# Shares of background conversion in a DeltaNet and feed-forward kernel, another PSUM ring for one unit's outputs, and another first activation

## The chip, the cores and the metric

The kernel runs on one core of a Trainium2 chip. It has five engines that matter here: PE (TensorE, matmuls), DVE (VectorE), ACT (ScalarE), POOL (GpSimd) and SP (SyncE, which only starts transfers here). Each runs its own instructions in order. The metric is the device time of one execution in microseconds (us), lower is better.

## What is computed

```python
# attention: q, k, v of (4, 8, 768, 48), beta of (4, 8, 768), float32
k_n = k / (np.linalg.norm(k, axis=-1, keepdims=True) + 1e-06)
for t in range(S):
    y[:, :, t] = np.einsum('bhd,bhde->bhe', q[:, :, t], state)
    v_old = np.einsum('bhde,bhd->bhe', state, kt)
    state = state + bt[:, :, :, None] * np.einsum('bhd,bhe->bhde', kt, vt - v_old)
# (B, H, S, D) -> (B*S, H*D) = (3072, 384), then the feed-forward
h = x @ w_in                                # w_in (384, 2048), float64
g = h * (1.0 / (1.0 + np.exp(-1.702 * h)))
out = g @ w_out                             # w_out (2048, 384), float64
```

The two weight matrices are given in double precision and converted to float32 by the kernel, as integer work on their raw words.

## The kernel before

The sequence is cut into 6 chunks of 128 positions; with 4 batches that makes 24 units. Within a chunk the recurrence is a triangular system: the kernel inverts its 32x32 diagonal blocks (`invert`, all on DVE) and solves the four blocks of a unit one after the other.

**Hops.** The first chunk's units 0 to 3 have no state yet. They are solved as two pairs, 0 and 1, then 2 and 3, in eight *hops* each (lines 1333 to 1342, the first run, and 1364 to 1370, the second run, whose hop 0 stands apart on line 1345). In a hop PE solves one block of one unit and multiplies what is already solved into the next block of the other; ACT copies both results out of PSUM; the next hop's PE work needs these copies. `gather` puts a unit's values into PSUM first. Between hops PE runs matmuls on constants (`warm`) or one step of the feed-forward (`feed`). `put_out` (line 1325) multiplies a unit's outputs (`queries`, `outputs`), has ACT copy them into `xT` (`leave`), and adds the new state on DVE (`state`).

**Conversion in the background.** Each piece of weight takes six operations (`conversion`, line 229): an AND on DVE, a Relu on ACT, then OR, another mask, and two multiplications on DVE. `conversions` interleaves a piece with the first operation of the next one. `fill(us)` (line 327) emits such operations until their planned costs (0.75, 0, 0.95, 0.7, 0.95, 0.95) reach the given sum. The costs are planned for 768 columns, as in the first pieces; later pieces have 512 or 384. The texts name the pieces by the kernel's own names: *in 0* to *in 3* and *in 6* to *in 11* are w_in, *out f* is rows f of w_out (out 4 and out 6 are pairs). After out 6 the same background generator emits `invert(1)`, the inversion for the next chunk, and then the rest of the conversions. Where a piece is finished, `fetches` may start the transfer of another one. The raw words of out 1 and out 2 are loaded by `fetch_out` on lines 1350 and 1351, after `put_out(pair[1])`; the transfers that bring the last rows into `xT` are issued in `copies` (line 805) and stand before them on SP.

**Order.** Instructions through `vec`, `act`, `pe`, `pool` and `sync` are pinned: they keep the program's order on their engine. Calls through `nc.gpsimd` and `nc.sync` may be placed freely.

**After the hops.** A loop of 25 steps (line 1397) has in each a `fill(1.0)` and one step of the feed-forward's first matrix for units 0 to 3 (`hidden`, six matmuls; every second step ends in one Gelu on ACT). At fixed steps it also normalizes keys of later units (`early`: a square on ACT, a sum on DVE, a power on POOL, a reciprocal on DVE, eight scalings on ACT). Then come the first eight row blocks of the second matrix (`both_written`), the wait for the inversion, and from line 1429 the slots: slot 3 solves unit 4's first block and takes the second half of `both_written`, which waits for converted pieces; slot 4 and all later ones follow.

**PSUM.** Before the slots the pools are `ps_moe` (ring *moe*: warm matmuls and the feed-forward), `ps_big`, `ps_seq` (ring *seq*) and `ps_acc` (ring *acc*), two banks each. `psV`, which `gather` fills, lies in *acc*.

Of the kernel before, what the change touches and what calls it, by code (L numbers as in the profile page):

```python
# [13 lines left out]
ACT = mybir.ActivationFunctionType  # L14
# [4 lines left out]
def kernel(  # L19
# [50 lines left out]
    ps_moe = ctx.enter_context(tc.tile_pool(name="ps_moe", bufs=2, space=PSUM))  # L70
    early_banks = ExitStack()
    ps_big = early_banks.enter_context(tc.tile_pool(name="ps_big", bufs=2, space=PSUM))
    ps_seq = early_banks.enter_context(tc.tile_pool(name="ps_seq", bufs=2, space=PSUM))
    ps_acc = early_banks.enter_context(tc.tile_pool(name="ps_acc", bufs=2, space=PSUM))
# [15 lines left out]
    def place(dst, n):  # L90

        return dst[n if n < B else n % 2] if dst is QP else dst[n % len(dst)]
# [3 lines left out]
    def segments(n):  # L96

        c, m = units[n]
        if n < B:
            return [(slice(0, C), m, slice(c * C, (c + 1) * C))]  # L100
        at = c * C + m // 2 * CH
        return [(slice(u * CH, (u + 1) * CH), m % 2 * 2 + u, slice(at, at + CH)) for u in range(2)]

    def load(n, pairs, dma=nc.sync.dma_start):
        for dst, src in pairs:
            for rows, b, t in segments(n):
                dma(  # L107
                    out=place(dst, n)[rows, :, 0:D],
                    in_=src[b, :, t, :].rearrange("h p d -> p h d"),
                )  # L110
# [24 lines left out]
    vec, act, pe, pool = Engine(nc.vector), Engine(nc.scalar), Engine(nc.tensor), Engine(nc.gpsimd)  # L135
# [11 lines left out]
    ident = cpool.tile([128, 128], F32, name="ident")  # L147
# [6 lines left out]
    def warm(n, after=None):  # L154
        ps = ps_moe.tile([128, 256], F32, tag="moe", name="ps_warm")
        if after is not None:
            after(ps[:, 0:1], 0.0)
        for _ in range(n):
            pe.matmul(ps, lhsT=ones[:, 0:128], rhs=ones, start=True, stop=True)

    table = cpool.tile([128, 1], F32, name="table")
    act.activation(table, ident[:, 0:1], ACT.Copy)

    w_out = cpool.tile([128, FC, DM], F32, name="w_out")

# [161 lines left out]
    def fill(us):  # L327
        while us > 0:
            us -= next(behind, us)
# [126 lines left out]
    def gram(n):  # L456

        return gram_whole(n) if n < B else gram_halves(n)
# [44 lines left out]
    def turn(n):  # L503
        kTs[n] = wk.tile([128, NP, 128], F32, tag="kT", name="kT", bufs=5)
        transposed(home(n), kTs[n])

    def load_diagonal(n, Nd, dma):

        b = units[n][1]
        dma(  # L510
            out=NT[b * NB * H : (b + 1) * NB * H].rearrange("d i k -> d (i k)"),
            in_=Nd.rearrange("(d r) -> d r", r=BS * BS),
        )
# [15 lines left out]
    def send_blocks(n, others=(), dma=sync):  # L529

        G = ready[n][2]
        Nd = dram.tile([H * C * BS], F32, tag="Nd", name="Nd", bufs=4)
        to = Nd.rearrange("(h p k) -> p h k", p=C, k=BS)
        for blk in range(NB):
            u = slice(blk * BS, (blk + 1) * BS)
            k = u if n < B else slice(blk % 2 * BS, (blk % 2 + 1) * BS)
            (beside if blk in others else dma)(out=to[u], in_=G[u, :, k])
        return Nd

    def load_diagonals(Nds):  # L540

        for b in range(B):
            load_diagonal(b, Nds[b], sync)
# [89 lines left out]
    def bank(name, shape=(128, H, D), big=False):  # L633
        if late:
            return one_bank(name)[:, 0 : H * D].rearrange("p (h d) -> p h d", h=H)
        from_, tag = (ps_big, "big") if big else (ps_seq, "seq")
        return from_.tile(list(shape), F32, tag=tag, name=name)
# [3 lines left out]
    class Step:  # L641
# [104 lines left out]
                )  # L746

        def queries(self):
            pool_, tag = (ps_acc, "acc") if self.n % 2 else (ps_seq, "seq")
            whole = [pool_.tile([128, 512], F32, tag=tag, name="psY") for _ in range(2)]  # L750
            self.psY = [w[:, 0:256].rearrange("p (s t) -> p s t", s=2) for w in whole]
            self.psS = whole[0][:, 256 : 256 + NP * D].rearrange("p (j d) -> p j d", j=NP)
            if self.c > 0:

                self.turned(
                    (0, 5, 4, 1, 2, 7, 6, 3),
                    lambda h: ST[self.rows(h), self.b, h // 2 * D : h // 2 * D + DP],
                    lambda h: self.QS[self.rows(h), h // 2, 0:128],
                    True,
                )  # L760
# [382 lines left out]
    def new_step(n):  # L1143
        if n >= len(units):
            return NoStep()
        steps[n] = (Step if n < B else Half)(n)
        return steps[n]

    def together(solves, belows):

        solves = [(X, blk) for X, blk in solves if X]
        belows = [(X, blk) for X, blk in belows if X]
        psU = bank("psU") if solves else None
        psRs = [bank("psR") if X.n >= B else None for X, blk in belows]
        for h in range(H):
            for X, blk in solves:
                X.solve(blk, h, psU)
            for (X, blk), psR in zip(belows, psRs):
                X.below(blk, h, psR)
        for X, blk in solves:  # L1160
            X.solved(blk, psU)
        for (X, blk), psR in zip(belows, psRs):
            X.rest(blk, psR)
# [133 lines left out]
    pair = [new_step(n) for n in range(B)]  # L1297
# [12 lines left out]
    Ndx = [send_blocks(n) for n in (B, B + 1)]  # L1310
# [6 lines left out]
    def hops(a, b):  # L1317

        yield [(a, 0)], []
        for blk in range(NB - 1):  # L1320
            yield [(b, blk)], [(a, blk)]
            yield [(a, blk + 1)], [(b, blk)]
        yield [(b, NB - 1)], []

    def put_out(s):
        s.queries()
        s.outputs(True, lambda: fill(1.7))
        steps.pop(s.n)

    path, later = hops(*pair[:2]), hops(*pair[2:])  # L1330
    for X in pair[:2]:
        X.gather()
    for i in range(2 * NB):
        together(*next(path))
        if i in (1, 3):
            turn(B + HB + i // 2)
        if i in (4, 5):
            gram(B + HB + i - 4)
            Ndx.append(send_blocks(B + HB + i - 4))
        if i < 2 * NB - 1:  # L1340
            warm(NU if i == 2 else NU // 2 if i in (1, 3, 4, 5) else 2 * NU // 3)
        fill(1.8)
    put_out(pair[0])
    load_diagonals(Ndx)
    together(*next(later))
    put_out(pair[1])
    for X in pair[2:]:
        X.gather()
    load(8, ((KN, k),), sync)
    for f in range(1, 3):  # L1350
        fetch_out(f)
# [5 lines left out]
    def feed(n=1):  # L1357
        for _ in range(n):
            while ffn and next(ffn[0], None) is None:
                ffn.pop(0)  # L1360
# [3 lines left out]
    for i in range(1, 2 * NB):  # L1364
        together(*next(later))
        if i < 4:
            warm(NU if i < 3 else NU // 2)
        if i > 2:
            feed()
        fill(1.8)  # L1370
    for s in pair[2:]:
        put_out(s)
        feed()
# [89 lines left out]
```

## Time and profile before

| | |
|---|---|
| median of 3 runs | 722.04 us (721.86 to 733.28) |
| the profiled execution, in all | 721.79 us |
| its span, first to last instruction | 720.1 us |
| mean granted PE clock over the span | 0.979 |
| busy PE, DVE, POOL, ACT | 678.0, 457.1, 256.1, 239.0 us |
| Gelu's table load, and the load at the start | 1.28 us each, at 98.11 and 0.80 us |
| first instruction of the background inversion | 126.53 us |

How to read it: times in the timeline are us from the first instruction. A line of the timeline gives the start, the length, the engine, the operation and its tiles as out<-in; in square brackets stands how long the engine had been idle and what released it. "PE busy" has modelled ends, so a busy PE may still wait a little. The profile gives line 123 for everything that is recorded through the helper `pinned`, so operations are told apart by their tiles: `VU<-psU` and `VU<-psV` are the two copies of a hop, `w_in<-w_in,low` or `w_out<-w_out,low` is the Relu of a conversion, and `raw` or the weight's own name as a source marks its other operations.

### The profile page before, as it was taken

How to read it: one execution, taken by the hardware profiler on the slowest of the kernel's cores; microseconds unless marked ns; L12 is line 12 of the kernel's file. 1: busy time of each engine (PE TensorE's matmuls, PEld its weight loads, DVE VectorE, ACT ScalarE, POOL GpSimd, SP SyncE). 2: the span in 40 equal slices, each digit the busy share in tenths (PEclk: the TensorE clock that was granted, in tenths of full speed). 3: DMA queues.
4: the chain of work that ended last, by engine and by line, in shares of the span. 5: the costliest groups of instructions: out<-in, count | busy, mean ns of one | idle time of the engine just before them, and what ended most of it. 6: DMA issues, size and time to landing. Idle time of an engine off the chain costs nothing.

```text
span 720.1 us, 20454 instructions
## 1 busy us (share of the span) xinstructions
PE 678.0 (94%) x8787; PEld 582.7 (81%) x8787; DVE 457.1 (63%) x869; ACT 239.0 (33%) x566; POOL 256.1 (36%) x267
## 2 busy tenths in 40 slices
PE   9289899987999999999999999999999999999997
PEld 7156788854568888898988988988988988989997
DVE  4799758996577498597597595795793892110000
ACT  2363565433233313323323333223323223122020
POOL 6085002310156652542642733623522403304032
PEclk9677999999999999999999999999999999999999
DMA  9896655224222313214114124223122111010100
GB/s 173 140 191 144 178 126 130 60 50 109 56 51 60 57 35 80 42 37 93 28 36 93 29 49 80 45 44 61 35 53 54 31 26 31 7 24 1 29 0 23
DMA packets 129179, 46.66 MB, mean 65 GB/s; under 512 B 118848, under 2 KB 123584, under 8 KB 129088
## 3 DMA queue, kind: packets, MB, share of 16 engines
q1 hardware_dynamic: 125280, 39.89, 27.2%
q0 software_dynamic: 2624, 5.07, 3.2%
q8 instruction: 69, 1.13, 0.7%
q10 hardware_dynamic: 1184, 0.39, 0.2%
q14 instruction: 22, 0.18, 0.1%
HBM read 33.13 MB, written 11.01 MB: 61 GB/s over the span
## 4 chain that ended last, share of the span: by engine, by line
PE 50%; DVE 32%; DMA 6%; issue 5%; ACT 4%; SPq 3%; POOL 0%; DVEq 0%; ACTq 0%; POOLq 0%
PE ph L123 22%; PE po L123 14%; DVE P L123 14%; DVE YB L123 7%; DVE NT L123 4%; PE four L123 4%; PE ps_warm L123 3%; PE psU L123 3%; DMA NT<-Nd 3%; DVE VU L123 2%; DVE w_out L123 2%; DMA Nd<-G 2%; PE psT L123 2%; SPq L123 2%; PE psR L123 1%
## 5 line engine op out<-in xcount | busy, mean ns | idle before, releaser
L123 PE MATMUL ph<-xT,w_in 128*128 128x256 f32 x1152 | 258.0, 381 | 0.0
L123 PEld LDWEIGHTS ph<-xT,w_in 128*128 128x128 f32 x1152 | 215.6, 190 | 30.4 <-DVE o L123 0.7
L123 PE MATMUL po<-w_out,gT 128*128 128x192 f32 (+1 forms) x720 | 139.7, 349 | 12.7 <-DVE o L123 5.4
L983 POOL TENSOR_TENSOR gT<-gT 128x512 f32<-128x512 f32 x80 | 105.1, 1323 | 102.7 <-ACT gT L123 68.1
L123 PEld LDWEIGHTS po<-w_out,gT 128*128 128x128 f32 x720 | 118.6, 191 | 26.7 <-issue 8.4
L123 DVE TENSOR_TENSOR P<-NT,YB 64x2 f32<-64x2 f32 (+9 forms) x200 | 124.0, 620 | 5.7
L123 ACT ACTIVATE gT<-ph 128x512 f32<-128x512 f32 x90 | 53.8, 598 | 143.4 <-PE ph L123 142.4
L123 DVE TENSOR_REDUCE YB<-P 64x2 f32<-64x2 f32 (+9 forms) x200 | 81.7, 409 | 6.9
L123 PE MATMUL po<-TW,gT 128*128 128x192 f32 x480 | 82.0, 328 | 0.8 <-ACT o L123 0.8
L123 PEld LDWEIGHTS po<-TW,gT 128*128 128x128 f32 x480 | 78.0, 190 | 1.8 <-ACT o L123 1.1
L849 POOL TENSOR_SCALAR_AFFINE_SELECT M<-M 64x512 f32<-64x512 f32 x40 | 29.9, 747 | 94.6 <-ACT M L123 93.4
L123 ACT COPY VU<-psU 32x384 f32<-32x384 f32 x96 | 45.2, 471 | 51.7 <-PE psU L123 42.0
L123 DVE TENSOR_TENSOR o<-o,po 128x192 f32<-128x192 f32 x40 | 13.8, 346 | 73.8 <-PE po L123 44.5
L123 DVE TENSOR_TENSOR VU<-VU,psR 32x384 f32<-32x384 f32 x40 | 22.1, 554 | 40.8 <-PE psR L123 40.1
L123 DVE TENSOR_TENSOR NT<-NT,bL 64x1024 f32<-64x1024 f32 (+1 forms) x9 | 12.0, 1333 | 46.7 <-DMA NT<-Nd 46.7
L107 POOL DMA_DIRECT2D KN<-in_k_dram x24 | 17.0, 712 | 68.7 <-PE four L123 68.7
L123 DVE TENSOR_TENSOR VU<-VU,four 128x384 f32<-128x384 f32 x19 | 10.5, 551 | 45.8 <-issue 33.3
L346 POOL TENSOR_TENSOR rn<-ssq,half 128x8 f32<-128x8 f32 x12 | 22.2, 1846 | 47.6 <-DVE ssq L123 47.6
L123 PEld LDWEIGHTS psU<-VU,XB 32*32 32x32 f32 x1536 | 27.4, 105 | 13.7 <-issue 9.4
L123 ACT COPY xT<-four 128x256 f32<-128x256 f32 (+1 forms) x40 | 13.2, 330 | 76.1 <-DVE ST L123 73.7
L123 PE MATMUL ps_warm<-ident 128*128 128x256 bf16 x235 | 35.3, 310 | 2.1 <-POOL low L123 1.4
L123 ACT COPY M<-four 128x512 f32<-128x512 f32 x19 | 11.2, 587 | 78.7 <-DVE VU L123 69.9
(133 smaller groups left out, 786.7 us busy)
## 6 DMA issues: line engine op xcount, KB each, us to landing
QP<-in_q_dram SPq DMA_DIRECT2D x40, 96.0 KB, 2.8
VU<-in_v_dram SPq DMA_DIRECT2D x40, 96.0 KB, 3.6
out_dram<-o SPq DMA_DIRECT2D x40, 96.0 KB, 2.2
raw<-in_moe_w_out_dram SPq DMA_DIRECT2D x9, 384.0 KB, 3.8
NT<-Nd SPq DMA_DIRECT2D x24, 128.0 KB, 2.7
XB<-Yd SPq DMA_DIRECT2D x24, 128.0 KB, 2.6
Yd<-NT SPq DMA_DIRECT2D x22, 128.0 KB, 2.1
Nd<-G SPq DMA_DIRECT2D x86, 32.0 KB, 1.7
```

Source lines behind the costliest of these rows:

```text
L107: dma(out=place(dst, n)[rows, :, 0:D], in_=src[b, :, t, :].rearrange("h p d -> p h d"),)
L123: return lambda *a, **kw: tc.keep_in_program_order(op(*a, **kw))
L346: nc.gpsimd.tensor_tensor(rn, ssq, half, op=ALU.pow)
L849: nc.gpsimd.affine_select(out=M, in_=M, compare_op=ALU.is_gt, fill=0.0, base=0, pattern=[[0, H], [1, CH]], channel_multiplier=-1,)
L983: (engine or nc.gpsimd).tensor_tensor(o, a, b, op=op)
```

## The change

Four edits:

- the first activation, on a one-column tile called `table`, is Gelu where it was Copy;
- unit 1's output banks come from the ring *moe* (unit 3's stay in *acc*, units 0 and 2's in *seq*);
- `gather` of units 2 and 3 stands before the second run's hop 0 and before unit 1's output, where it stood behind both;
- `fill` is asked for 2.1 in each hop of the first run (1.8 before), for 2.7 in each of the hops 1 to 7 of the second run (1.8 before), and for 1.9 on each side of the second run's hop 0 (nothing before).

```diff
-    act.activation(table, ident[:, 0:1], ACT.Copy)
+    act.activation(table, ident[:, 0:1], ACT.Gelu_apprx_sigmoid)
...
         def queries(self):
-            pool_, tag = (ps_acc, "acc") if self.n % 2 else (ps_seq, "seq")
+            pool_, tag = (
+                (ps_moe, "moe") if self.n == 1 else (ps_acc, "acc") if self.n == 3
+                else (ps_seq, "seq")
+            )
...
             warm(NU if i == 2 else NU // 2 if i in (1, 3, 4, 5) else 2 * NU // 3)
-        fill(1.8)
+        fill(2.1)
     put_out(pair[0])
-    load_diagonals(Ndx)
-    together(*next(later))
-    put_out(pair[1])
     for X in pair[2:]:
         X.gather()
+    load_diagonals(Ndx)
+    fill(1.9)
+    together(*next(later))
+    fill(1.9)
+    put_out(pair[1])
     load(8, ((KN, k),), sync)
     for f in range(1, 3):
         fetch_out(f)
...
         if i > 2:
             feed()
-        fill(1.8)
+        fill(2.7)
     for s in pair[2:]:
         put_out(s)
         feed()
```

## The prediction, made before the changed kernel was run

> **What bounds it now.** I first cut the span into five stages with the busy-time table (stretch, length, then busy us of PE, weight load, DVE, ACT and POOL, granted clock, DMA share, GB/s).
>
> ```profile
> 0.00:65.20 65.20, 45.63 (x389) 34.71 (x389) 50.51 (x103) 26.27 (x63) 36.48 (x67) 0.79 0.92 170
> 65.20:110.07 44.87, 42.01 (x964) 33.83 (x963) 29.86 (x53) 27.10 (x57) 1.42 (x2) 1.00 0.57 139
> 110.07:162.03 51.96, 48.74 (x300) 38.32 (x297) 47.61 (x98) 24.70 (x67) 13.13 (x10) 1.00 0.36 80
> 162.03:185.97 23.94, 17.87 (x136) 9.64 (x136) 16.65 (x37) 7.09 (x13) 1.42 (x2) 0.93 0.35 90
> 185.97:720.00 534.03, 523.74 (x7005) 466.18 (x7004) 312.43 (x579) 153.80 (x366) 203.61 (x188) 1.00 0.21 43
> ```
>
> Stage two is the hops, three the feed-forward's first half beside the inversion, four the wait for the last conversions. From 185.97, where slot 4 solves, PE is busy 98%: the change touches nothing there, so a shift at slot 4 should arrive whole at the end. Stages three and four leave PE idle 3.2 + 6.1 = 9.3 us; that, and DVE's 15.0 idle us of stage two, are what earlier conversion could use.
>
> Then the chain of waits, stages two and three (start, length):
>
> ```profile
> 97.63 0.47 ACT VU L123
> 98.11 1.28 ACT L123
> 99.41 0.61 ACT gT L123
> 100.03 0.47 ACT VU L123
> ...
> 126.53 1.23 DVE NT L123
> ```
>
> The nameless step is Gelu's table load, ahead of two copies of the hops. At 126.53 the inversion starts; until 162 DVE's chain leads.
>
> Last, the timeline by engine, for what a hop waits on. ACT, DVE, SP, and the landing time of the first of the two `raw` loads:
>
> ```profile
> 69.66 0.60 ACT L123 ACTIVATE kT<-psT 128x512 f32<-128x512 f32 x1
> 70.64 0.48 ACT L123 COPY VU<-psU 32x384 f32<-32x384 f32 x1 [0.39 <-PE psV L123]
> 71.02 0.47 ACT L123 COPY VU<-psV 32x384 f32<-32x384 f32 x1
> 71.62 0.73 ACT L123 ACTIVATE w_in<-w_in,low 128x512 int32<-128x512 int32 x1
> ...
> 71.17 0.41 DVE L123 TENSOR_SCALAR w_in<-gT 128x512 int32<-128x512 int32 x1
> ...
> 87.29 3.77 SPq L123 DMA_DIRECT2D xT<-last  x6
> 91.15 1.80 SPq L123 DMA_DIRECT2D KN<-in_k_dram  x2
> 93.00 1.09 SPq L123 DMA_DIRECT2D raw<-in_moe_w_out_dram  x2
> DMA to landing us min/median/max: 3.9/3.9/3.9
> ```
>
> Each conversion has one Relu on ACT, between DVE's first and second operation, and ACT runs in order with the hop's copies. DVE lags PE here: the operation that feeds this Relu ends at 71.58, though the hop's solve was over at 70.56.
>
> **The change, part by part.** I counted `fill`'s planned costs through the program for both versions, which gives the operations in each hop, and laid the four queues out with the durations of these rows. The old order laid out so reaches slot 4 within 1.5 us of the trace; below, trace times plus the difference.
>
> *First run of hops, 2.1 for 1.8.* The Relu of piece in 6 moves from hop 2 into hop 1, ahead of hop 2's copies. It can't start before 71.62 and takes 0.73, so the copies start at 72.4, not 70.64: 1.7 later, of which 0.35 was slack behind the warm matmuls: +1.4. Two later Relus cost 0.2. Put-out 0 starts 1.6 late.
>
> *Gather, ring and the two fills of 1.9.* The gather's 1.5 us are only moved; its wait for unit 1's copies (0.64 in the trace) goes, as unit 1's outputs now hold the other ring. In its place two Relus stand ahead of the second run's hop 0 copy (0.7) and of unit 1's leaving copies (1.2), each waiting for DVE. The warm matmuls of its hop 1, which share that ring, now wait for unit 1's state sum on DVE: queued behind them is hop 2's solve, 1.4 to 2.2 late. The leaving copies come 3.2 late.
>
> *The fetch.* Those copies release the six `xT` transfers on SP, and behind them stand KN and the two `raw` loads of w_out rows 1 and 2: 5.7 us from the first to the `raw` load, by the rows. So it issues at 96.2 instead of 93.0 and lands 3.9 later, at 100.1. Before, piece out 1 was first touched at 102.54, long after landing. Now the 2.7 of the second run's hop 2 asks for it at 94.2: DVE stands 5.9 us, its Relu 5.7, and the copies of the second run's hop 3, queued behind on ACT, start at 101.1 instead of 94.38. PE sits 4.0 us. This is the largest term; if the data were there it would be nothing, so 0 and +4.0 are its ends. I take 4.0, for every step of it has a row.
>
> *The table.* Loaded at the start, where one load of 1.28 stands already. ACT ran Relu, Square and Copy after the second load without a third, so that set holds them. It saves 1.28 on ACT, of which about 0.8 stays on this path. The Trainium skill (ScalarE: Activation LUTs, What ACT_TABLE_LOAD costs) prices a switch at about 2.66 us, 1.38 of it a drain; here Gelu starts 0.02 after the load, so the trace shows no drain behind it. By the Trainium skill's figure the forecast would be some 1.4 us lower.
>
> *End of the hops:* unit 2 leaves at 112.6 instead of 106.77, **+5.8**.
>
> *The inversion.* By then the conversions are eleven us further. From 100.1 DVE has 17.1 us of operations left before the inversion (the ends of out 0 and 1, 2.35 each for out 2 and 3, 4.1 for each pair, state sums), 1.2 of collisions with POOL's subtractions (the 128x768 row at 118.00 took 1.38 against 0.69 elsewhere) and 2.0 of waits for Relus: start at 120.5, **6.0 earlier**.
>
> *But PE needs that less.* From 115.9 PE has its 25 remaining hidden steps (1.3 each, 36 matmuls took 7.77) whatever DVE does. And the early normalizations keep their places in the loop, now behind the inversion: unit 8's reciprocal comes after ten of its steps, 120.5 + 7.4 + 0.5 = 128.4, where ACT scaled at 119.79 before. Behind its 1.93 stands a Gelu that frees PE's bank: PE waits 2.5 us at the second hidden layer; other waits shrink by 0.4. Last Gelu: 150.75 + 5.8 + 2.1 = 158.7. Eight pairs of products (10.0) bring slot 3's solve to 169.3, where 162.03 was set by the inversion: **+7.3**.
>
> *The second half* had 23.94 us, most of it PE waiting for conversions. Now pieces 8, 13, 9 and 10 are done; four are left, the first behind a Relu queued after slot 3's copies. 2.9 for solve, copies and Relu; 9.1 for the rest of four conversions, 1.6 for two V sums, 1.6 of waits; 3.0 from the last conversion to slot 4 as before: 18.2, **-5.7**.
>
> Sum: +7.3 - 5.7 = +1.6 at slot 4. The profiled execution took 721.79 (span 720.1 and 1.7 around it), the median 722.04: **723.5**.
>
> **Rivals.** *The data is there (720.0).* If SP reaches the loads earlier, or `fill`'s work falls a step later than I counted, DVE never stands. The hops end at +2.0, inversion starts 10 early, slot 3 solves at 165.5 and slot 4 at 184.0: -2.0. For it: SP had a wait inside those rows that I can't place. 0.27.
>
> *Conversions fit the hops' gaps (714).* If no Relu delays a copy, the gather's wait and the table come off (0.6 + 0.8), inversion starts ten us earlier, and most of the 9.3 idle us of PE is collected: 6 to 8 in all. Against it: the row at 71.17. 0.15.
>
> *PE goes cold (727).* In the first stage PE stopped at 21.4 and the granted clock fell to 0.50 from about 24.5; after idling between 166 and 172 it was 0.50 in 172 to 174. A 4.0 us stand at 98 to 102 lies beyond the 3.1 that sufficed. Half clock for 3.5 us (as there) to 7 us (as after 35) costs 1.7 to 3.5 in matmul-bound hops: 725.2 to 727. It decides from a stand of about 3 us with no warm matmul in it. The Trainium skill (TensorE: Matmul & The Clock Gate, Part 1) says the clock halves after at least one idle window of about 3.4 us whose phase runs free. By that rule the trace agrees, and 4.0 us would only sometimes hold a whole window. Short matmuls around the stand speak against it. 0.18.
>
> That the change doesn't do what it says is possible for the table alone, worth 0.8.
>
> **Numbers.** Forecast 0.40, the rivals as given. The range runs from 715, near the collected case, to 729: 727 and 2 for what the layout misses (its error on the old order was 1.5). A difference of 2%, 14.4 us, is about what a measurement can tell from no change; none of the cases reaches it, the best by 6 us and the worst by 9. Unseen effects, such as SP transfers that are placed freely in the slots: 0.04 faster, 0.91 within, 0.05 slower.
>
> **What would show it.** One table load, at the start. The first run's hop 2 copies near 72.4; the `raw` loads on SP near 96; a stand of DVE and ACT of 5 to 6 us on out 1; the second run's hop 3 copies near 101. Inversion near 120.5 and slot 3 near 169: if it solves by 163 the third stage was mis-sized. Slot 4 at 187 to 188 and 534 us behind it. Wrong altogether if stage five changes length by over 2 us.

## The result, and the profile after

| | before | after |
|---|---|---|
| median | 721.86 us | 729.28 us |
| lowest | 719.22 us | 725.92 us |
| profiled execution, in all | 721.79 us | 727.72 us |
| its span, mean granted clock | 720.1 us, 0.979 | 726.0 us, 0.971 |

The medians are over 20 executions each. The ratio is 1.0112, with a 95% interval of 1.0078 to 1.0146: slower by 7.4 us by the medians and by some 8 by the ratio, where 1.5 were forecast, and just outside the range. Nearly every kernel of this case has some executions that lie 5 to 15 us above its lowest, with a lower mean granted clock, how many they are differs from kernel to kernel, and the ratios leave the longest of them out.

First the busy time by stage, cut at the same events as before (the hops' first solve, the hidden step behind unit 3's output, the solves of slots 3 and 4), with the same columns:

```profile
0.00:63.83 63.83, 43.42 (x390) 33.63 (x390) 49.58 (x102) 26.19 (x63) 35.35 (x67) 0.79 0.91 171
63.83:118.39 54.56, 45.58 (x963) 36.15 (x963) 39.55 (x70) 28.27 (x60) 4.06 (x4) 0.91 0.54 132
118.39:171.72 53.33, 49.14 (x300) 38.21 (x296) 43.19 (x93) 22.96 (x65) 11.13 (x8) 1.00 0.41 88
171.72:192.30 20.58, 17.29 (x138) 9.49 (x137) 12.55 (x27) 5.84 (x11) 1.54 (x2) 0.92 0.17 49
192.30:726.00 533.70, 524.12 (x7005) 466.26 (x7004) 312.41 (x579) 153.49 (x366) 203.79 (x188) 1.00 0.21 43
```

The hops (second row) grew by 9.7 us, and of that only 3.6 is PE work; the rest PE stood. The granted clock there is 0.91 where it was 1.00. The third row grew by 1.4, the fourth shrank by 3.4, the fifth is the same within 0.4 us. So the loss is in the hops, and the gain in the fourth stage does not pay for it.

The chain of waits in the second run of hops (start, length):

```profile
95.66 4.93 DMA raw<-in_moe_w_out_dram
100.61 0.37 DVE w_out L123
101.00 0.62 ACT w_out L123
101.64 0.47 ACT VU L123
...
104.16 2.86 PE ph L123 x6
...
122.56 1.23 DVE NT L123
```

This is the predicted path link by link: the late load of out 1, DVE's first operation on it, its Relu, and only then the copies of hop 3. New is the last-but-one link: a hidden step of six matmuls took 2.86 us, and the six of the next step took 1.49 at 107.95. The timeline of DVE and ACT shows how long each stood (in brackets), and of SP when the load was issued:

```profile
100.61 0.36 DVE L123 TENSOR_SCALAR w_out<-raw 128x384 int32<-128x384 int32 x1 [7.31 <-DMA raw<-in_moe_w_out_dram]
101.00 0.62 ACT L123 ACTIVATE w_out<-w_out,low 128x384 int32<-128x384 int32 x1 [7.96 <-DVE w_out L123]
101.64 0.47 ACT L123 COPY VU<-psU 32x384 f32<-32x384 f32 x1
...
95.66 1.09 SPq L123 DMA_DIRECT2D raw<-in_moe_w_out_dram  x2
```

Why matmuls took twice as long is in the windows of 2 us (same columns as the stages; the clock is the third figure from the end):

```profile
68.00:70.00 2.00, 0.65 (x48) 0.65 (x52) 1.97 (x3) 1.87 (x4) 0.00 (x0) 0.93 0.18 24
70.00:72.00 2.00, 2.00 (x38) 1.45 (x29) 1.97 (x4) 0.71 (x1) 0.00 (x0) 0.50 0.63 118
72.00:74.00 2.00, 2.00 (x55) 1.34 (x53) 1.93 (x4) 0.85 (x3) 0.00 (x0) 0.72 1.09 312
...
98.00:100.00 2.00, 0.00 (x0) 0.00 (x0) 0.00 (x0) 0.00 (x0) 0.00 (x0) 1.00 1.03 336
100.00:102.00 2.00, 0.00 (x0) 0.00 (x0) 1.36 (x4) 0.97 (x2) 0.00 (x0) 0.61 1.27 146
102.00:104.00 2.00, 1.34 (x48) 1.31 (x48) 1.93 (x6) 0.58 (x2) 0.00 (x0) 0.50 0.94 251
104.00:106.00 2.00, 2.00 (x11) 1.55 (x6) 0.23 (x1) 0.84 (x2) 0.99 (x1) 0.50 0.64 215
```

From 98 to 100 no engine works while transfers run, and PE, which stands until 102.7, restarts at half clock, which lasts to about 107. The same happens on a smaller scale at 70 to 73, in the first run of hops: PE had stood 1.63 us ahead of hop 2's matmuls, behind a Relu (which one, a section below shows). In the profile before, all rows from 66 to 110 have 1.00.

### The profile page after: what moved, and what is told of

The parts are those of the page before. It is cut to its first block, busy times and chain, and to the rows that moved or that the text cites. A ratio compares the mean times of both kernels' runs of the same rounds, so it can differ in the third digit from the quotient of the medians.

```text
span 726.0 us, 20454 instructions
## 1 busy us (share of the span) xinstructions
PE 679.5 (94%) x8787; PEld 583.7 (80%) x8787; DVE 457.3 (63%) x869; ACT 236.8 (33%) x565; POOL 255.9 (35%) x267
## 4 chain that ended last, share of the span: by engine, by line
PE 50%; DVE 30%; DMA 7%; issue 4%; ACT 4%; SPq 2%; POOL 2%; DVEq 0%; ACTq 0%; POOLq 0%
PE ph L123 21%; PE po L123 16%; DVE P L123 12%; DVE YB L123 6%; PE four L123 4%; DVE NT L123 3%; DMA NT<-Nd 3%; PE psU L123 3%; PE ps_warm L123 3%; DVE VU L123 2%; DVE w_out L123 2%; PE psT L123 2%; DMA Nd<-G 2%; PE psR L123 1%; SPq L537 1%
## 5 line engine op out<-in xcount | busy, mean ns | idle before, releaser
L123 PE MATMUL psU<-VU,XB 32*32 32x48 f32 x1536 | 33.7, 204 | 7.9 <-ACT VU L123 7.9
```

Source lines behind the costliest of these rows:

```text
L123: return lambda *a, **kw: tc.keep_in_program_order(op(*a, **kw))
```

## The experiments

Edits are against the changed kernel where nothing else is said. Each ratio is to the kernel before, run beside it on the same chip, where its median lay between 720.76 and 722.07. A figure from a profile is that of one execution.

### The late load

**Loads early.** The two `raw` loads are issued behind `load_diagonals`, ahead of the second run's hop 0 and of the `xT` transfers:

```diff
     load_diagonals(Ndx)
+    for f in range(1, 3):
+        fetch_out(f)
     fill(1.9)
...
     load(8, ((KN, k),), sync)
-    for f in range(1, 3):
-        fetch_out(f)
```

> The changed kernel, with only the two raw loads of out 1 and out 2 issued before unit 1's output instead of behind it. Theory (the loads come late on SP, DVE and with it ACT and PE stand for them, and PE's clock drops during the stand): the DVE wait of 7.3 us on the raw load is gone, the copies of the second run's hop 3 start near 94.5 instead of 101.6, unit 2's leaving copies near 105 instead of 115.1, no half clock between 96 and 108, slot 4 solves 4 to 7 us earlier than 192.3, and the time is 721 to 724. Rival (the Relus that stand ahead of the hop copies and the normalizations behind the inversion cost it, the stand is made up later anyway): slot 4 within 2 us of 192.3 and 726 to 729.

Measured: 725.17 us, ratio 1.0019 (0.9978 to 1.0060). The stand on out 1 is gone: no operation of DVE waits for it any more. Five of twelve executions took 718.9 to 719.9, two us less than the kernel before's usual ones; the other seven took 724.8 to 729.5. The profiled one (728.82) is of the second sort, and its windows show where it lost:

```profile
72.00:74.00 2.00, 0.72 (x20) 0.43 (x20) 1.97 (x4) 1.56 (x3) 0.00 (x0) 1.00 0.94 208
74.00:76.00 2.00, 2.00 (x56) 1.68 (x46) 1.93 (x5) 1.23 (x3) 0.00 (x0) 0.78 0.54 137
76.00:78.00 2.00, 2.00 (x55) 1.47 (x57) 1.69 (x3) 0.92 (x2) 0.00 (x0) 0.50 0.98 310
```

PE stood 1.27 us ahead of hop 3 in the first run of hops, the clock fell to 0.50, and it stayed there to about 95, with PE listed as fully busy. So the load is about 4 us of the loss by the medians (nearer 7 by the ratios), and a fall of the clock in the first run is a second one.

**Second run's fill back.** `fill(2.7)` in the second run is 1.8 again.

> The changed kernel with the second run's hops back at 1.8. Out 1 is then asked for later, so the stand should shrink to 2 us or less by either theory; but fewer pieces are done. Late-loads theory: hops end 3 to 5 us earlier than in the changed kernel, the inversion starts 1 to 3 us later than 122.6, and the second half of the output products is as long as in the old kernel (near 24 us instead of 20.6): time 725 to 729. If the amount of conversion in the hops is itself what costs (the rival), it is at the old kernel's 722 or below.

Measured: 734.24, ratio 1.0123 (1.0080 to 1.0165): no better, and outside the 725 to 729 that were expected. In the profiled execution, which is the longest of the twelve (740.24), the stand did not go, it moved one hop on: the load is issued at 101.18 and DVE takes it up at 107.34. That execution lost the clock twice, at 75 to 92 and from 109 to about 123. Asking for less in the second run is not a cure while the load comes after the `xT` transfers.

**First run's fill back**, loads still late:

```diff
-        fill(2.1)
+        fill(1.8)
     put_out(pair[0])
```

> The changed kernel with the first run's fill back at 1.8, all else kept, the late loads too. Theory (the Relu ahead of the first run's hop copies is what lets the clock fall at 70 to 76, and with six operations fewer done by then DVE comes to piece out 1 later): copies of hop 2 near 70.6, clock 1.00 in 64:90, a stand of DVE on the load of 1 to 4 us instead of 7.3, slot 4's solve 2 to 4 us before the changed kernel's 192.3, and the time at 724 to 726. Rival (the fill of the first run costs nothing by itself, the late load is all): the stand stays at 5 to 7 us and the time stays at 728 to 729.

Measured: 724.54, ratio 1.0025 (0.9993 to 1.0057). The granted clock is 1.00 from 64 to 100, and DVE's stand is half as long, with the load issued at 93.32 and 4.4 us to landing:

```profile
97.68 0.36 DVE L123 TENSOR_SCALAR w_out<-raw 128x384 int32<-128x384 int32 x1 [3.64 <-DMA raw<-in_moe_w_out_dram]
```

Behind its shorter stand the clock fell too (0.57 from 100 to 104). Slot 4 solves at 185.95, 6.3 sooner than in the changed kernel, where 2 to 4 were expected; but this execution (720.86) is among the shorter ones of a kernel with median 724.54, so 6.3 may be more than the edit gives on average. The rival, that this fill costs nothing by itself, is out.

### The clock

**Warm matmuls in the stand.** Only PE's idle time before hop 3's copies is filled:

```diff
-            warm(NU if i < 3 else NU // 2)
+            warm(NU if i < 3 else 40)
```

> The changed kernel with 40 warm matmuls (5.0 us) instead of 6 after the second run's hop 3: PE is busy through most of the stand, which stays as it is. If the half clock costs time of its own: no granted clock of 0.5 between 100 and 108, unit 2's leaving copies 1.5 to 3 us earlier than 115.1, time 1.5 to 3 us below the changed kernel, and fewer runs near 734. If the cold clock is hidden under other waits: the same time within 1 us, or slower by up to 1 us where the warm matmuls outlast the stand.

Measured: 727.65, ratio 1.0045 (1.0003 to 1.0086); six executions at 721.5 to 724.6, six at 730.7 to 734.8. The profiled one (723.80) still has the stand of DVE (6.18 us) and the fall at 70 to 73, but no half clock behind the stand:

```profile
100.00:102.00 2.00, 0.61 (x29) 0.41 (x31) 1.93 (x5) 1.49 (x3) 0.00 (x0) 1.00 1.31 181
102.00:104.00 2.00, 2.00 (x44) 1.50 (x37) 1.12 (x3) 0.85 (x3) 0.76 (x1) 1.00 1.01 293
104.00:106.00 2.00, 2.00 (x38) 1.68 (x36) 0.77 (x2) 1.95 (x4) 0.23 (x1) 1.00 0.76 288
```

Hop 3's copies start at 100.57 (101.64), unit 2 leaves at 111.90 (115.09). From the one to the other it takes 11.33 us, against 13.45 in the changed kernel: the half clock behind the stand costs 2.1 us, alone. The rows of the changed kernel add up to the same: 1.4 in the hidden step (2.86 for 1.49), the rest in the hops' own matmuls.

**Warm matmuls in hop 1 of the first run**, on top of the early loads:

```diff
-            warm(NU if i == 2 else NU // 2 if i in (1, 3, 4, 5) else 2 * NU // 3)
+            warm(NU if i == 2 else 18 if i == 1 else NU // 2 if i in (3, 4, 5) else 2 * NU // 3)
```

> The changed kernel with the loads early, 2.1 still in the first run, and 18 warm matmuls in its hop 1 where there were 6, which fill the 1.6 us that PE stood there. Theory (that stand is what lets the clock fall): granted clock 1.00 in 64:100, at most 3 of 12 executions above 723 where seven of twelve were without the warm matmuls, median 719 to 721. Rival (the fall comes from elsewhere, such as the later gaps of the same hops, or the two groups of times have another cause): five or more of 12 at 724 to 730, median above 722.

Measured: 721.06, ratio 0.9989 (0.9953 to 1.0025); three of twelve above 723, where seven were without them; clock 1.00 in every row from 64 to 100. The extra matmuls fill PE's stand ahead of hop 2, and as hop 2 then comes later, the stand ahead of hop 3 is 0.94 us and not 1.27. That agrees with the theory, but the interval overlaps that of the early loads alone (0.9978 to 1.0060), so the difference of 4 us between the two is likely, not proved. A pair below points the same way.

### One part alone

**The kernel before with 2.1 in the first run:**

```diff
-        fill(1.8)
+        fill(2.1)
     put_out(pair[0])
```

> The kernel before with the first run's fill at 2.1 and nothing else. Theory: its hop 2 copies come 1 to 1.7 us later, PE idles as much, the granted clock falls to 0.50 near 72 to 76 as in the changed kernel, the lower group of times is 1 to 2 us above the kernel before's (722.5 to 723.5) and half of the runs or more lie 5 to 8 us higher: median 723 to 729. Rival (the drop at 70 to 76 belongs to the table or the ring, not to the fill): clock 1.00 in 64:90, median 721.5 to 723.5 with as few high runs as the kernel before.

Measured: 723.46, ratio 1.0022 (1.0003 to 1.0040). By the ratio the first fill alone costs about 1.6 us (0.2 to 2.9), and four of its twelve executions took 732.7 to 736.2. In the profiled one (724.05) the clock falls at the same place as in the changed kernel:

```profile
68.00:70.00 2.00, 0.89 (x61) 0.89 (x64) 1.93 (x4) 1.63 (x4) 0.00 (x0) 0.88 0.13 19
70.00:72.00 2.00, 2.00 (x25) 1.38 (x18) 1.97 (x4) 0.93 (x2) 0.00 (x0) 0.50 0.71 164
```

So the fall here needs neither the table nor the ring. But this profile does not show the fill to be its cause either. The Relu ahead of this stand is not the one that 2.1 moves (that one starts at 71.05 here); it stands at the same place in the kernel before. Relu and first matmul of hop 2, before and then changed:

```profile
67.84 0.94 ACT L123 ACTIVATE w_in<-w_in,low 128x768 int32<-128x768 int32 x1 [1.27 <-DVE w_in L123]
69.69 0.23 PE L123 MATMUL psU<-VU,XB 32*32 32x48 f32 x1 [0.58 <-ACT VU L123]
...
67.51 0.94 ACT L123 ACTIVATE w_in<-w_in,low 128x768 int32<-128x768 int32 x1 [2.32 <-DVE w_in L123]
69.35 0.23 PE L123 MATMUL psU<-VU,XB 32*32 32x48 f32 x1 [1.63 <-ACT VU L123]
```

What differs is when the hops begin: at 65.20 in the profile of before, at 63.83 in that of the changed kernel and at 63.55 here, while DVE, which this Relu waits for, comes only 0.3 to 0.6 sooner. Over the profiles of all kernels the hops begin at 63.55 to 66.17, and the four with a stand over 1.6 us here began at 63.55 to 64.06; one of them has a fill of 1.8.

The stand that 2.1 does make lies one hop later, behind the Relu that it moves. It is 1.27 to 1.28 us in the profiles of the early loads, of the second run's fill back and of the fill of 17 below, and in all three the clock fell there, at about 75, and stayed at 0.50 until 92 to 95. Those hops began at 64.72 to 66.17. The first run's fill back to 1.8, with hops from 65.77, has no stand ahead of hop 3 and kept 1.00. So this second, longer fall does go with the fill.

In the profile of this section the clock fell once more, from 86 to 93, with no stand of PE over 0.67 us just before.

**The kernel before with Gelu's table loaded first:**

```diff
-    act.activation(table, ident[:, 0:1], ACT.Copy)
+    act.activation(table, ident[:, 0:1], ACT.Gelu_apprx_sigmoid)
```

> The kernel before with Gelu as the first activation and nothing else. Theory (the prediction's term): the load at 98.11 is gone, the copies behind it come 1.2 us sooner, hops end 0.5 to 1.0 us sooner, and DVE's chain to the inversion takes up most of it, so the median is 0 to 0.8 below the kernel before's. Rival (the Trainium skill, ScalarE: Activation LUTs, What ACT_TABLE_LOAD costs, 2.66 a switch): 1.5 to 2.5 below.

Measured: 720.63 against 720.76, ratio 1.0001 (0.9979 to 1.0024). No gain can be told from zero, and the interval reaches to 1.5 below at best. The Trainium skill (ScalarE: Activation LUTs, What ACT_TABLE_LOAD costs) gives 2.66 us for a switch; nothing like it came back here, and in the trace of before Gelu started 0.02 after a load of 1.28, with no drain between.

**Table, ring and gather alone** (all fills as before: 1.8, none, 1.8):

```diff
-        fill(2.1)
+        fill(1.8)
...
-    fill(1.9)
     together(*next(later))
-    fill(1.9)
...
-        fill(2.7)
+        fill(1.8)
```

> The changed kernel with all three fills back at the old sizes: only the table load, unit 1's ring and the gathers' place are left of the change. Theory (these three help a little, the fills cost): hops end 1 to 1.5 us earlier than in the old kernel, slot 4 at 184 to 185, time 719.5 to 721.5. Rival (the ring makes the warm matmuls wait for unit 1's state sum and this costs): 722 to 725.

Measured: 722.99, ratio 0.9994 (0.9956 to 1.0031). These three edits are worth nothing that can be told from zero. The profiled execution (724.45) shows a wait that the kernel before does not have: the first hidden step waits 1.32 us for `xT`, and the clock is 0.76 and 0.56 in the two windows of 5 us from 95 on.

### The second half

In the changed kernel DVE does nothing from 165.8 to 174.75; the next conversion's Relu stands behind slot 3's copies on ACT. The last fill ahead of the slots is asked for three conversions more:

```diff
     for n in (2 * B, 2 * B + 1):
         load_diagonal(n, Nds[n], sync)
-    fill(4)
+    fill(17)
```

> The changed kernel with nothing but the last fill ahead of the slots at 17 where it was 4. Theory (the change's conversions are further on, but between 165.8 and 174.75 DVE does nothing, and what was saved can't be collected behind slot 3's copies): the stand on the load and the half clock around 100 to 107 stay as they are, slot 3 solves near 171 to 172, the second half takes 15 to 16.5 us instead of 20.58 with no wait of PE for a conversion, the lower group of times is 722 to 725, the median 4 to 5.5 below the changed kernel's 729.28, at 723.5 to 725.5. Rival (the gain of 17 needs the earlier loads): second half 19 us or more, median 727 to 729.

Measured: 727.89, ratio 1.0093 (1.0059 to 1.0126); the median fell by 1.4, not by 4 to 5.5. In the profiled execution (726.89) the second half is 15.31 us (177.08 to 192.39) instead of 20.58, as the theory said, but the clock was at 0.50 from 75 to 92 and slot 3 came 5.4 later. The shorter half is there; in this execution the loss ahead of it takes back all of it. Why the median gained so little is open: the lowest execution (725.23) is only 0.7 below the changed kernel's, and no execution without that long fall was profiled.

The same edit on the version with early loads and 1.8 in the first run (described below):

> The version with the loads early and 1.8 in the first run, and the last fill ahead of the slots asked for 17 where it was 4: some three conversions move in front of slot 3's copies, into the 9.46 us in which DVE stood there. Theory (the second half saved less than the prediction's 5.7 because DVE came to it with idle time in front and four conversions behind slot 3's copies): slot 3 still solves near 161, three conversions of 2.35 are gone from the second half, PE no longer stands 0.6 to 1.2 before each product nor runs them at half clock, the half takes 16 to 18 us instead of 21.4, and the time is 711 to 713. Rival (the half is bound by something else, the loads of the last pieces or PE's own 17 us): 20 us or more, 715.5 to 716.5.

Measured: 713.25, ratio 0.9886 (0.9833 to 0.9940), below that version by 3.3 us by the medians, by 5.3 by the ratios. PE's timeline from slot 3's solve to slot 4's:

```profile
162.68 0.87 PE L123 MATMUL psU<-VU,XB 32*32 32x48 f32 x32
163.48 0.66 PE L123 MATMUL psT<-ident,QP 128*128 128x128 f32 x4
163.97 4.04 PE L123 MATMUL po<-w_out,gT 128*128 128x384 f32 x12
167.94 0.87 PE L123 MATMUL psR<-VU,G 32*32 32x48 f32 x32
168.74 4.14 PE L123 MATMUL po<-w_out,gT 128*128 128x384 f32 x12
172.80 1.00 PE L123 MATMUL four<-QS,kT 48*64 48x112 f32 x32
173.73 4.33 PE L123 MATMUL po<-w_out,gT 128*128 128x384 f32 x12
177.99 0.88 PE L123 MATMUL psU<-VU,XB 32*32 32x48 f32 x64
```

No line has a bracket: PE no longer waits, and 15.31 us is what its own work takes. The 16 to 18 that I expected left room for waits that did not come.

### The version that beats both

**Loads early and 1.8 in the first run:** the edits of the first and third experiments together. Of the change stay the table, the ring, the gather, the two fills of 1.9 and the 2.7.

> The same with the two raw loads ahead of the second run's hop 0 as well: table, ring, gather, the two fills of 1.9 and the 2.7 are all that is left of the change. Theory: neither the drop of the clock in the first run nor a stand on the load; the inversion starts near 117, slot 4 solves 1 to 2 us before the 185.97 of the kernel before, undisturbed executions take 718.5 to 720.5, and fewer of them belong to the higher group of times than the seven of twelve with 2.1 in the first run. Rival (the higher group comes from elsewhere, the 2.7 of the second run for one): again about half of the runs at 724 to 729, median over 722.

Measured: 716.57, ratio 0.9960 (0.9936 to 0.9985), nine of twelve at 715.4 to 718.5. The inversion starts at 114.49 and slot 4 solves at 182.33; both are better than expected. What it leaves is the idle DVE of the section above:

```profile
163.96 0.56 DVE L123 SCALAR_TENSOR_TENSOR w_out<-raw,w_out 128x384 int32<-128x384 int32 x1 [9.46 <-ACT w_out L123]
```

**And 17 ahead of the slots, and 18 warm matmuls in hop 1:** the edits above together.

> All repairs together: loads early, 1.8 in the first run, 17 ahead of the slots, and 18 warm matmuls in hop 1 of the first run. Theory: granted clock 1.00 in 64:100, where the version without the extra warm matmuls had 0.50 in 70:72; lowest runs as there (710 to 712), at most 2 of 12 above 716, median 710.5 to 712.5, ratio near 0.986. Rival (the warm matmuls only delay the hops): lowest runs 1 us higher, as many above 716 as without them (2 of 6), median 713 to 715.

Measured: 711.92, ratio 0.9863 (0.9826 to 0.9901), all six executions at 711.2 to 713.2. The version without the extra warm matmuls ran at 710.1 to 720.6 (six executions). The two profiles differ in the row after the place where PE stood. Without them:

```profile
68.00:70.00 2.00, 0.30 (x27) 0.30 (x31) 1.97 (x3) 1.95 (x4) 0.00 (x0) 0.99 0.13 16
70.00:72.00 2.00, 2.00 (x62) 1.55 (x50) 1.97 (x4) 1.19 (x4) 0.00 (x0) 0.50 0.60 74
```

With the extra warm matmuls:

```profile
68.00:70.00 2.00, 2.00 (x60) 1.66 (x60) 1.97 (x3) 1.68 (x4) 0.00 (x0) 1.00 0.67 152
70.00:72.00 2.00, 2.00 (x67) 1.61 (x57) 1.93 (x5) 1.51 (x3) 0.00 (x0) 1.00 0.84 274
```

With 1.8 PE stood even longer here (1.74 us ahead of hop 2) than with 2.1 in the changed kernel (1.63). So the fall goes with PE's stand, whatever makes it: ahead of hop 2 it is an early start of the hops, ahead of hop 3 the fill of 2.1.

## Why the prediction was wrong, step by step

**The path was right.** One table load is left; the `raw` load was issued at 95.66 (96.2), DVE stood 7.31 and ACT 7.96 us, of which 5.9 and 5.7 were foreseen, hop 3's copies came at 101.64 (101.1). The first run's hop 2 copies came at 72.03 (72.4). The early loads took the stand away, and in the five lower executions the loss with it: 719.7 in their middle, where the rival in which the data is there said 720.0. None of these five was profiled, so it is the time that agrees, and its steps are not shown.

**The step that failed: the stand and the cold PE were set against each other.** The forecast took the stand of 4.0 us at full clock and gave the cold PE a chance of 0.18 as a rival. But the rival needs only the stand, which was the forecast's own largest term: PE stood from 96.4 to 102.7, and the half clock came on top. Its price of 1.7 to 3.5 was good: 2.1, by the warm matmuls in the stand. It belonged in the sum.

The limit that the prediction gave it, a stand of about 3 us, was also wrong, and its own trace spoke against it. It read the second fall of before as one after idling from 166 to 172; PE worked in between, and the stand in which the clock fell was 1.81 us:

```profile
170.00:172.00 2.00, 0.45 (x1) 0.45 (x2) 1.92 (x5) 0.00 (x0) 0.00 (x0) 0.82 0.00 0
...
171.55 5.96 PE L123 MATMUL po<-w_out,gT 128*128 128x384 f32 x12 [1.81 <-DVE w_out L123]
```

PE's stand was 6.3 us and not 4.0 because hop 2's solve, which was to come 1.4 to 2.2 late, was on time (91.32 for 91.27): the warm matmuls ahead of it ran at 89.83, before the state sum (90.14) that they were to wait for. This changed no end time, since hop 3's copies waited for the load either way.

With the half clock in the sum, the profiled execution closes. Unit 2 leaves at 115.09, 2.5 later than predicted: 2.1 of half clock, and 0.5 by which the copies of hop 3 were late, since the load took 4.9 to land and not 3.9 but was issued 0.5 sooner. From there to slot 3's solve it takes 56.6, and 56.7 were predicted. The inversion at 122.56 (120.5) is late by no more than the hops, and its worth was put rightly: PE did not need it sooner.

**The second half was mis-sized**, 20.58 for 18.2. From the last conversion to slot 4 it took 4.4 us and not the 3.0 that the trace of before has: PE stood 1.89 ahead of the last eight products and ran them in 4.41, where the same eight took 3.04 before. The windows of the changed kernel show the clock:

```profile
188.00:190.00 2.00, 2.00 (x5) 1.13 (x6) 1.64 (x5) 0.74 (x2) 0.00 (x0) 0.80 0.00 0
190.00:192.00 2.00, 2.00 (x4) 0.67 (x2) 0.00 (x0) 0.22 (x1) 0.00 (x0) 0.50 0.54 197
```

In the profiles of the early loads and of the warm matmuls in hop 1 the same stand of 1.89 left the eight products at 3.04, so this 1.4 belongs to the execution and not to the change. The four conversions with the V sums and waits between them took 13.2 (174.75 to 187.90), not 12.3. So slot 4 is 6.3 late, not 1.6: the difference of 4.7 is 2.5 in the hops and 2.4 here, less 0.1 between. Stage five is 0.3 shorter, as foreseen within 2 us.

**The first run's clock was in no step.** The clock came up sooner at the start, so the hops began at 63.83 and not 65.20, which is luck of this execution and gained little: PE then stood 1.63 us ahead of hop 2, since DVE came only 0.3 sooner. The copies of hop 2 hang on DVE, as forecast, so the early start hardly moved them. In the stand the clock fell, and twelve warm matmuls took 2.74 for 1.48; but most of that lay beside the wait for hop 2's copies, which ended at 72.88, 0.3 ahead of hop 3's first matmul. The long fall ahead of hop 3 costs more. The fill of 17 has the changed kernel's program up to the slots, and in its profile, with that fall, slot 3 came 5.4 later. Some of the changed kernel's executions must have the like: its median is 1.6 above the profiled execution. That these are the eight above 732 is likely; none of them was profiled.

**The rival of fitting conversions** (714, chance 0.15) was out for this kernel, but its aim was within reach: with the loads early, PE kept warm and the idle 9 us of DVE used, the same work ends at 711.92.

What stays open: why a fall of the clock ends after 3 to 4 us in one execution and after 17 or more in another of nearly the same order. In the first run the four short falls came ahead of hop 2, with the twelve warm matmuls in a row right behind, and the three long ones ahead of hop 3, with short matmuls and rows of six behind. That this decides is not tested.

## What to carry to other kernels

When a step of a forecast lets PE stand, price the clock with it, in the same sum, also for short stands (here 1.3 us was enough). When background work is brought forward, move its loads first and look at which transfers stand ahead of them on the queue. And look for idle time of the background engine just ahead of the stage that waits for it: here one number there (17 for 4) gave 3 to 5 us.

## What the runs showed of the hardware

The granted clock fell to 0.50 when PE had stood 1.3 to 1.7 us in the first run of hops (0.65, 0.72 and 0.30 us busy in a window of 2), though 1.27 did not always do it: the version with early loads and 1.8 had 0.73 busy and kept 1.00. In the kernel before with 2.1 it fell near 87 behind two windows with 1.32 and 1.36 busy. The Trainium skill (TensorE: Matmul & The Clock Gate, Part 1) names at least one idle window of about 3.4 us; by these rows less is enough. It also says that about 3.4 us of sustained work release the clock. After the stand at 98 to 102 that agrees (1.00 again from about 107), but with the early loads alone it stayed at 0.50 from 76 to about 95 while every row had PE busy 2.00 of 2.00 us, by modelled ends.

The same two loads of 384 KB took from 3.1 us (early loads) to 6.8 us (second run's fill back) to land. An early issue does not make them quick: in the version with the fill of 17 and early loads they took 5.5 to 5.9.
